# Computing the last 128 columns of a down projection transposed, with the weight stationary

## The chip, the cores and the metric

The kernel runs on one core of a Trainium2 chip. The metric is device time in microseconds (us) of one execution. A core has TensorE (matmuls; in the profile PE, and PEld for the loads of the stationary operand), VectorE (DVE), ScalarE (ACT), GpSimd (POOL) and SyncE (SP), each with an instruction queue of its own that is worked through in order, and 16 DMA engines. In this kernel nearly all DMAs are issued from SP's queue. TensorE writes to PSUM, which has 8 banks of 512 f32 columns; an instruction that needs what another engine makes waits on a semaphore.

## What is computed

Two branches over the same 2048 tokens of 640 columns are mixed by a gate per token. In outline (H = 32 heads of 20 columns):

```python
q, k, v = split(x @ wqkv)                       # per head
phi(t) = concat(softmax(t @ w_phi), softmax(-(t @ w_phi)))
num = phi(q) @ (phi(k)^T @ v);  den = phi(q) @ sum(phi(k))
a = concat_heads(num / (den + 1e-6)) @ wo
b = (silu(x @ w_gate) * (x @ w_up)) @ w_down    # 640 -> 1728 -> 640
g = sigmoid(sum(x * gate_w))
out = g * a + (1 - g) * b
```

The change is in how `b`'s last product, with `w_down`, is computed.

## The kernel before

**Tiling.** Tokens come in 16 tiles of 128 (`t`) and 4 blocks of 512 (`bt`). The 1728 inner columns of the feed-forward branch are 14 chunks of 128 (`k`; the last has 64).

*Gate and up* (`ffn`, lines 668 to 686): for a chunk and a block, five matmuls of 512 moving columns each for gate and for up, with the weight stationary and the transposed tokens `xT` moving. `ffn_tail` (640 to 666) turns them into `hT` (chunk on the partitions, tokens along the row): a tanh and a scaled copy `us` on ACT (line 456), a step on DVE (659), a product on POOL (665). `hT` has two buffers, one for even and one for odd blocks.

*Down* (`down`, lines 768 to 787): for each token tile, `hT`'s 128 tokens are stationary and `w_down` (`wd`) moves. The output is 640 columns wide, over two PSUM banks, so each of the 14 chunks is passed twice: 14 matmuls of 512 columns, then 14 of 128 columns. A down tile holds a pair of banks. The last tile's two parts are two tasks, so that the first can be finished while the second runs.

```python
        def part(j):
            return acc(bank(ctx["ps"], j, 0, P if j else 512),
                       [(hT[:, hb, k, tk], wd[:, k, 512:D] if j else wd[:, k, 0:512]) for k in range(NK)])
```

*K tiles and Q tiles* (`features`, 851 to 936): projections of a token tile (matmuls with `wkv` or `wq`), then per head a maximum and a minimum, two subtractions (lines 899 to 911, DVE), an exponential (ACT), a sum and a reciprocal (922, 926, DVE) and a normalization (932, POOL). K tiles feed `kvpart` (matmuls of `v1` and `phi`). A Q tile (`qtile`, 991 to 1039) goes on: a transposing DMA from SP (`qT`, phi to `eT`), a product with the summed keys and values (`num`, 11 narrow matmuls), a division on DVE (`den`, `o`: lines 1015, 1017, 1025), a transposing DMA (`oT`), and the product with `wo` (ten matmuls, half of them 128 columns wide).

*Output* (`finish`, `finals`, 730 to 766): the two branches meet in `xsb`, bf16. The one that comes first is scaled into `xsb` on ACT, for tiles below `B_FIRST` = 8 the feed-forward branch and from there on the attention branch. The second is added: for tiles below `FIN_DVE` = 12 by a scaled copy to `xb` on ACT (`evac`) and an add on POOL (`plus`, line 763), from tile 12 on by one DVE operation from PSUM (`fin`, line 749). Then SP issues the store of the tile. For the last tiles the down matmuls themselves wait for the first branch's store (line 745: `parts[0][0].deps.append(store_t[t])`).

**The order of work** is written by a planner when the kernel is built (`_Plan`, lines 236 to 337). Each piece of work is a task with an engine, a planned duration, a latency (`LAT`, line 246, the time until another engine may use it), dependences, a priority (lower goes first) and the buffers it takes and gives back (PSUM banks or pairs, `xb`, `eT`, `oT` and others). Whenever an engine is free in the plan, the task of lowest priority number that is ready and has its buffers is issued; it is never taken back. The engines then run their queues in that order, with semaphore waits. The planned durations set the order alone.

```python
    L_SLACK, E_SLACK, O_SLACK = 1.0, 1.8, 1.6
    K_AT, K_EACH, Q_AT, Q_EACH = 29.00, 6.158, 120.27, 8.184
```

`E_SLACK` and `O_SLACK` are added to the planned landing of a `qT` and an `oT` transfer; the second line says how early a K or Q tile's first matmul may stand in the plan. For TensorE `num` has priority 1, `wo` 1.5, K tiles 3, Q tiles 5; gate, up and down tiles have 10 and more and fill what is left, in the order of the list `seq` (lines 1051 to 1062): in blocks 2 and 3 the four down tiles of the block before are put one by one behind the gate and up pairs from the sixth on; the last two down tiles of block 2 are put behind all gate and up pairs (`late`), and the four of block 3 at the end.

Of the kernel before, what the change touches and what calls it, by code (L numbers as in the profile page):

```python
# [6 lines left out]
P = 128  # L7
S_TOK = 2048
D = 640
# [231 lines left out]
class _Plan:  # L241
# [11 lines left out]
    def add(self, eng, cost, fn, deps=(), prio=5.0, lat=None, acq=(), rel=(), name=""):  # L253
        t = _Task(eng, cost, fn, deps, prio, self.LAT[eng] if lat is None else lat,
                  tuple(acq), tuple(rel), len(self.tasks), name)
        self.tasks.append(t)
        return t
# [82 lines left out]
def _mm(*cols):  # L340
    return sum(c / 2400.0 + 0.003 for c in cols)


def _build(
# [22 lines left out]
    def sb(name, shape, dtype):  # L367
        t = nc.alloc_sbuf_tensor(name, list(shape), dtype)
        tr.reg_tensor(t, "sbuf", nc.lookup_mloc(t).addr, rowelems(shape), mybir.dt.size(dtype))
        return t  # L370

    def sbat(name, shape, dtype, at):
        t = nc.alloc_sbuf_tensor_at(name, list(shape), dtype, offset=at)
        tr.reg_tensor(t, "sbuf", at, rowelems(shape), mybir.dt.size(dtype))
        return t
# [8 lines left out]
    hT = sb("hT", [P, 2, NK, 512], BF16)  # L384
    us = sb("us", [P, 3, 512], BF16)
    phi = sb("phi", [P, NPHI, NG, P], BF16)
    v1 = sb("v1", [P, 8, VW], BF16)
    eT = sb("eT", [P, 2, NG, P], BF16)
    olab = nc.alloc_sbuf_tensor("olab", [P, 2 * OW + 2 * D], BF16)
    obase = nc.lookup_mloc(olab).addr  # L390
# [26 lines left out]
    x2 = A_x[0]  # L417
    out2 = out[0]

    plan = _Plan({"bank": 8, "phi": NPHI, "st": 3, "eT": 2, "ob": 2, "oT": 2, "us": 3, "dn": 2, "xb": 2, "pp": 2})  # L420
    add = plan.add

    def bank(i, j, c0, c1, r0=0, r1=P):
        return ps[r0:r1, (2 * i + j) * 512 + c0:(2 * i + j) * 512 + c1]
# [4 lines left out]
    def wide(i, n=D):  # L429
        return ps[:, 2 * i * 512:2 * i * 512 + n]  # L430
# [19 lines left out]
    def acc(o, pairs):  # L450
        n = len(pairs)
        return [(o, l, r, i == 0, i == n - 1) for i, (l, r) in enumerate(pairs)]

    def actop(o, i, func, scale=1.0):
        reads = [i] + ([scale] if isinstance(scale, bass.AP) else [])
        run("act", lambda: act.activation(o, i, func, scale=scale), reads=reads, writes=[o])  # L456
# [4 lines left out]
    def poolop(fn, reads, writes):  # L461
        run("pool", fn, reads=reads, writes=writes)
# [7 lines left out]
    def dma(eng, dst, src, transpose=False, keep=False):  # L470
        eobj = tr.engobj[eng]
        reads = [src] if src.tensor.name in tr.addr else []
        writes = [dst] if dst.tensor.name in tr.addr else []
        fn = (lambda: eobj.dma_start(dst, src, transpose=True)) if transpose else (lambda: eobj.dma_start(dst, src))
        ev = run(eng, fn, reads=reads, writes=writes, semname="dma")
        if keep:
            out_evs.append(ev)
# [151 lines left out]
    gate_t = {}  # L629
    mult_t = {}  # L630
    down_t = {}

    def w_dep(k):
        col = P * k
# [33 lines left out]
    def ffn(bt, k, rank):  # L668
        tsl = slice(512 * bt, 512 * bt + 512)
        ctx = {}  # L670
        before = [down_t.get((bt - 2, u)) for u in range(4)]
        w_ = w_dep(k)
        if k == 13:
            gu = add("pe", _mm(*[512] * 5), lambda: mms(acc(one(ctx["g"], 0, 512),
                      [(wg[:, c, 1664:1792], xT[:, c, tsl]) for c in range(5)])),
                      deps=before + [xl[bt], wgl[NPC], wul[NPC]], prio=rank, acq=[("bank", ctx, "g")], name="gu")
            ffn_tail(bt, k, ctx, (gu, gu), 0)
            return
        g_ = add("pe", _mm(*[512] * 5), lambda: mms(acc(one(ctx["g"], 0, 512),
                 [(wg[:, c, P * k:P * k + P], xT[:, c, tsl]) for c in range(5)])),  # L680
                 deps=before + [xl[bt], wgl[w_]], prio=rank, acq=[("bank", ctx, "g")], name="gate")
        u_ = add("pe", _mm(*[512] * 5), lambda: mms(acc(one(ctx["u"], 0, 512),
                 [(wu[:, c, P * k:P * k + P], xT[:, c, tsl]) for c in range(5)])),
                 deps=[wul[w_]], prio=0.0, acq=[("bank", ctx, "u")], name="up")
        u_.after = g_
        ffn_tail(bt, k, ctx, (g_, u_), 0)
# [40 lines left out]
    pend = []  # L727
    wq_done = [None]

    def finish(t, which, ctx, dep):  # L730
        sc = gs[:, 0 if which == "a" else 1, t:t + 1]
        x_ = xsb[:, t, :]
        rel = [("pair", ctx, "ps")]
        if (t < B_FIRST) == (which == "b"):
            store_t[t] = add("act", 0.69, lambda: actop(x_, wide(ctx["ps"]), ACTF.Copy, scale=sc),
                             deps=[dep, gs_t[t // 4], wq_done[0]], prio=1, rel=rel, name=which + "st")
        else:
            pend.append((t, sc, ctx, dep, rel))

    def finals():  # L740
        for t, sc, ctx, dep, rel in pend:
            x_ = xsb[:, t, :]
            if t >= FIN_DVE:
                parts = dep if isinstance(dep, list) else [(dep, 0, D)]
                parts[0][0].deps.append(store_t[t])
                for d_, c0, c1 in parts:
                    def fin(x_=x_[:, c0:c1], ctx=ctx, sc=sc, c0=c0, c1=c1):
                        p_ = wide(ctx["ps"], c1)[:, c0:c1]
                        dveop(lambda: dve.scalar_tensor_tensor(out=x_, in0=p_, scalar=sc, in1=x_, op0=ALU.mult, op1=ALU.add),  # L749
                              [p_, sc, x_], [x_])  # L750
                    f = add("dve", 0.14 + 0.00105 * (c1 - c0), fin, deps=[d_, store_t[t], gs_t[t // 4]], prio=0.5,
                            rel=rel if c1 == D else (), name="fin")
                    add("sp", 0.33, lambda x_=x_, t=t, c0=c0, c1=c1: dma("sp", out2[t * P:(t + 1) * P, c0:c1], x_[:, c0:c1], keep=True),
                        deps=[f], prio=1, name="out")
                continue
            else:
                dep.deps.append(store_t[t])
                e = add("act", 0.69, lambda ctx=ctx, sc=sc: actop(xb[:, ctx["xb"], :], wide(ctx["ps"]), ACTF.Copy, scale=sc),
                        deps=[dep, gs_t[t // 4]], prio=1, acq=[("xb", ctx, "xb")], rel=rel, name="evac")

                def plus(x_=x_, ctx=ctx):
                    b_ = xb[:, ctx["xb"], :]
                    poolop(lambda: pool.tensor_tensor(x_, x_, b_, ALU.add), [x_, b_], [x_])
                f = add("pool", 1.35, plus, deps=[e, store_t[t]], prio=0.5, rel=[("xb", ctx, "xb")], name="plus")
            add("sp", 0.33, lambda x_=x_, t=t: dma("sp", out2[t * P:(t + 1) * P, :], x_, keep=True),
                deps=[f], prio=1, name="out")

    def down(bt, u, rank):
        t = 4 * bt + u
        ctx = {}  # L770
        hb = bt % 2
        tk = slice(P * u, P * u + P)

        def part(j):
            return acc(bank(ctx["ps"], j, 0, P if j else 512),
                       [(hT[:, hb, k, tk], wd[:, k, 512:D] if j else wd[:, k, 0:512]) for k in range(NK)])
        hold = {"deps": [mult_t[bt, k] for k in range(NK)] + wd_l, "prio": rank, "acq": [("pair", ctx, "ps")], "name": "down"}
        if t < NT - 1:
            d_ = add("pe", _mm(*([512] * 14 + [128] * 14)), lambda: mms(part(0) + part(1)), **hold)
            down_t[bt, u] = d_  # L780
            return t, ctx, d_
        first = add("pe", _mm(*[512] * 14), lambda: mms(part(0)), **hold)
        second = add("pe", _mm(*[128] * 14), lambda: mms(part(1)), prio=0.0, name="down")
        second.after = first
        down_t[bt, u] = second
        return t, ctx, [(first, 0, 512), (second, 512, D)]

    def premult(which, wT_l, prio, step=0.0, at=0.0):  # L790
        ev = []
# [260 lines left out]
    seq += [("f", k, 0) for k in range(K_PAIRS, NK)]  # L1052
    for bt in range(1, NBT):
        ks = list(range(K_PAIRS if bt == 1 else 0, NK))
        ds = [("d", u, bt - 1) for u in range(4)]
        for i, k in enumerate(ks):
            seq.append(("f", k, bt))
            if i >= D_AFTER and ds:
                seq.append(ds.pop(0))
        seq += ds  # L1060
    late = [e for e in seq if e[0] == "d" and e[2] == NBT - 2][2:]
    seq = [e for e in seq if e not in late] + late + [("d", u, NBT - 1) for u in range(4)]
    downs = []
    for i, (kind, j, bt) in enumerate(seq):
        if kind == "f":
            ffn(bt, j, 10.0 + 0.01 * i)
        else:
            downs.append(down(bt, j, 10.0 + 0.01 * i))
    for t in range(NT):
# [57 lines left out]
```

## Time and profile before

| what | value |
|---|---|
| median of 3 runs | 286.96 us (286.87 to 287.4) |
| the profiled execution's own time | 287.4 us |
| its span, first to last instruction | 285.7 us |
| granted TensorE clock | 1.000 |
| down matmuls (line 446, `ps<-wd,hT`) | 224 of 512 columns, 224 of 128 columns |
| issue to landing, median: `eT`, `oT` transposes | 3.6 us, 2.6 us |

Lines of the profile read like this: start or group, engine (PE, PEld, DVE, ACT, POOL, SPq for SP's DMA issues), source line, operation, output<-input by the program's names, shapes as partitions x elements, and a count. A matmul's recorded length includes its way through the array; matmuls follow each other more closely than that, so the distance of two starts is what one costs. Matmuls all carry line 446 and many ACT operations line 456, since a helper records them; tiles' names tell them apart. In the page's second part each digit is a 40th of the span, in tenths.

### The profile page before, as it was taken

To read this page: it belongs to the slowest core of one execution; us is meant where nothing else is said; L and a number is where in the kernel's file an instruction comes from. 1 tells how busy PE (TensorE), PEld (TensorE's weight loads), DVE (VectorE), ACT (ScalarE), POOL (GpSimd) and SP (SyncE) were. 2 spreads that over 40 slices of the span, in tenths; PEclk is the share of its full clock that TensorE was granted. 3 is DMA by queue.
4 is the path that set the end of the run, shared out by engine and by line. 5 is a ranking of instruction groups with operands and counts; after the bars stand their busy time and mean duration, and the time that the engine had idled before them with its cause. 6 is when DMAs were issued, how large, how long until landed. Compare 5 with 4: busy or idle time off the path is not lost.

```text
span 285.7 us, 5001 instructions
## 1 busy us (share of the span) xinstructions
PE 282.5 (99%) x1970; PEld 149.6 (52%) x1970; DVE 223.4 (78%) x318; ACT 149.1 (52%) x238; POOL 171.6 (60%) x168
## 2 busy tenths in 40 slices
PE   8999999999999999999999999999999999999996
PEld 3445554555554555654455656555554555555654
DVE  1323449998999797799999999999979979962312
ACT  2455655886676564436636444566664653562210
POOL 5099633749478635456784485589898458638100
PEclk9999999999999999999999999999999999999999
DMA  7979997920000000000002483744375245363211
GB/s 171 271 120 246 214 245 129 334 86 0 0 2 0 0 2 0 2 0 2 0 2 52 76 125 77 109 112 94 69 144 70 55 83 118 70 76 73 71 46 46
DMA packets 68112, 24.22 MB, mean 85 GB/s; under 512 B 56249, under 2 KB 68089, under 8 KB 68089
## 3 DMA queue, kind: packets, MB, share of 16 engines
q1 hardware_dynamic: 67433, 23.91, 40.1%
q8 instruction: 15, 0.25, 0.4%
q10 hardware_dynamic: 656, 0.00, 0.1%
q14 instruction: 8, 0.07, 0.1%
HBM read 8.30 MB, written 2.62 MB: 38 GB/s over the span
## 4 chain that ended last, share of the span: by engine, by line
PE 99%; DVE 0%; issue 0%
PE ps L446 97%; PE ps L619 2%; DVE xsb L749 0%
## 5 line engine op out<-in xcount | busy, mean ns | idle before, releaser
L665 POOL TENSOR_TENSOR hT<-hT,us 128x512 bf16<-128x512 bf16 (+1 forms) x56 | 64.1, 1154 | 53.1 <-DVE hT L659 31.1
L932 POOL TENSOR_TENSOR phi<-phi,rc 128x1320 bf16<-128x1320 bf16 x32 | 77.6, 2426 | 28.8 <-DVE rc L926 26.0
L446 PE MATMUL ps<-xT,wg 128*128 128x512 bf16 x280 | 69.7, 381 | 0.0
L446 PE MATMUL ps<-xT,wu 128*128 128x512 bf16 x260 | 64.3, 379 | 0.0
L446 PE MATMUL ps<-wd,hT 128*128 128x512 bf16 (+1 forms) x448 | 63.0, 299 | 0.0
L922 DVE TENSOR_REDUCE sm<-phi 128x66 f32<-128x1320 bf16 x32 | 48.5, 1519 | 10.6 <-ACT phi L456 10.6
L659 DVE SCALAR_TENSOR_TENSOR hT<-hT,ps 128x512 bf16<-128x512 bf16 (+1 forms) x56 | 37.6, 676 | 22.8 <-ACT hT L456 22.7
L456 ACT ACTIVATE hT<-ps 128x512 bf16<-128x512 f32 (+1 forms) x56 | 33.2, 597 | 40.7 <-PE ps L446 40.3
L456 ACT ACTIVATE phi<-phi 128x1320 bf16<-128x1320 bf16 x32 | 41.7, 1304 | 22.2 <-DVE phi L911 22.2
L446 PEld LDWEIGHTS ps<-wd,hT 128*128 128x128 bf16 x448 | 35.0, 98 | 27.4
L446 PE MATMUL ps<-wkv,xT 128*128 128x289 bf16 (+2 forms) x240 | 45.8, 343 | 0.0
L456 ACT ACTIVATE us<-ps 128x512 bf16<-128x512 f32 (+1 forms) x56 | 33.2, 597 | 16.4 <-PE ps L446 14.2
L446 PEld LDWEIGHTS ps<-xT,wu 128*128 128x128 bf16 x260 | 25.3, 98 | 30.8 <-ACT phi L456 0.4
L446 PEld LDWEIGHTS ps<-xT,wg 128*128 128x128 bf16 x280 | 26.0, 98 | 27.9 <-issue 1.5
L446 PEld LDWEIGHTS ps<-wkv,xT 128*128 128x128 bf16 x240 | 22.9, 97 | 18.4
L899 DVE TENSOR_REDUCE mx<-ps 128x33 f32<-128x660 f32 x32 | 26.6, 833 | 3.4 <-PE ps L446 3.3
L911 DVE TENSOR_TENSOR phi<-mn,ps 128x660 bf16<-128x660 f32 x32 | 26.4, 824 | 0.3
L903 DVE TENSOR_REDUCE mn<-ps 128x33 f32<-128x660 f32 x32 | 26.5, 828 | 0.0
L907 DVE TENSOR_TENSOR phi<-ps,mx 128x660 bf16<-128x660 f32 x32 | 26.5, 827 | 0.0
L456 ACT ACTIVATE xsb<-ps,gs 128x640 bf16<-128x640 f32 x16 | 12.7, 793 | 24.7 <-PE ps L446 24.7
L446 PE MATMUL ps<-wq,xT 128*128 128x512 bf16 (+1 forms) x160 | 24.3, 299 | 0.0
L446 PE MATMUL ps<-wo,oT 128*128 128x512 bf16 (+1 forms) x160 | 24.3, 299 | 0.0
(47 smaller groups left out, 184.9 us busy)
## 6 DMA issues: line engine op xcount, KB each, us to landing
out_dram<-xsb SPq DMA_DIRECT2D x15, 160.0 KB, 1.8
wd<-in_B_w_down_dram SPq DMA_DIRECT2D x1, 2080.0 KB, 9.3
wg<-in_B_w_gate_dram SPq DMA_DIRECT2D x2, 400.0 KB, 5.3
wu<-in_B_w_up_dram SPq DMA_DIRECT2D x2, 400.0 KB, 6.5
wo<-in_A_wo_dram SPq DMA_DIRECT2D x1, 800.0 KB, 10.0
wg<-in_B_w_gate_dram SPq DMA_DIRECT2D x2, 320.0 KB, 4.7
wu<-in_B_w_up_dram SPq DMA_DIRECT2D x2, 320.0 KB, 5.6
wkv<-in_A_wqkv_dram SPq DMA_DIRECT2D x1, 600.0 KB, 4.4
```

The costliest lines, as they stand in the source:

```text
L446: last = pe.matmul(o, lhsT=l, rhs=r, start=st, stop=sp_, skip_group_check=True)
L456: run("act", lambda: act.activation(o, i, func, scale=scale), reads=reads, writes=[o])
L619: last = pe.matmul(one(b, 0, 512), lhsT=ones_row[:, 0:P], rhs=ones_row[:, 0:512], start=True, stop=True, skip_group_check=True)
L659: dveop(lambda: dve.scalar_tensor_tensor(out=hap, in0=hap, scalar=1.0, in1=g_, op0=ALU.add, op1=ALU.mult), [hap, g_], [hap])
L665: poolop(lambda: pool.tensor_tensor(hap, hap, u_, ALU.mult), [hap, u_], [hap])
L899: dveop(lambda: dve.tensor_reduce(a, b, AX.X, ALU.max), [b], [a])
L903: dveop(lambda: dve.tensor_reduce(a, b, AX.X, ALU.min), [b], [a])
L907: dveop(lambda: dve.tensor_tensor(o_, a, b, ALU.subtract), [a, mx[:, ctx["st"], :]], [o_])
L911: dveop(lambda: dve.tensor_tensor(o_, a, b, ALU.subtract), [b, mn[:, ctx["st"], :]], [o_])
L922: dveop(lambda: dve.tensor_reduce(a, b, AX.X, ALU.add), [b], [a])
L932: poolop(lambda: pool.tensor_tensor(a, a, b, ALU.mult), [a, r], [a])
```

## The change

The 128 columns 512 to 639 of the down projection are taken out of the down tiles. For each block a new TensorE task `rest` computes them transposed: the 128-column slice of `wd` is stationary and 512 tokens of `hT` move, 14 matmuls into one bank. ACT copies the result to `xb` as bf16 (`rcp`), SP issues a transposing DMA of four 128x128 blocks (`turn`), which for blocks 0 and 1 goes straight to `xsb` and is scaled there by the gate on POOL (`rsc`), and for blocks 2 and 3 to a new buffer `rX`, from which a DVE operation of 128 columns per tile (`more`) adds it. `rX` shares its memory with `v1`. A down tile now has 14 matmuls of 512 columns, in one bank; the last tile's two parts are 384 and 128 columns wide. Copies, adds and finals of the feed-forward branch shrink from 640 to 512 columns. The last tile's columns 512 to 639 are stored by a DMA of their own. `rest` stands ahead of its block's down tiles in `seq`, and `hT` is free for block `bt` only when `rest` of `bt - 2` is done too. The planner's constants stay.

```diff
@@ -384,7 +384,11 @@
     hT = sb("hT", [P, 2, NK, 512], BF16)
     us = sb("us", [P, 3, 512], BF16)
     phi = sb("phi", [P, NPHI, NG, P], BF16)
-    v1 = sb("v1", [P, 8, VW], BF16)
+    vlab = nc.alloc_sbuf_tensor("vlab", [P, 8 * VW], BF16)
+    vbase = nc.lookup_mloc(vlab).addr
+    assert vbase % 32 == 0, vbase
+    v1 = sbat("v1", [P, 8, VW], BF16, vbase)
+    rX = sbat("rX", [P, 2, 4, P], BF16, vbase)
     eT = sb("eT", [P, 2, NG, P], BF16)
     olab = nc.alloc_sbuf_tensor("olab", [P, 2 * OW + 2 * D], BF16)
     obase = nc.lookup_mloc(olab).addr
@@ -417,7 +421,7 @@
     x2 = A_x[0]
     out2 = out[0]
 
-    plan = _Plan({"bank": 8, "phi": NPHI, "st": 3, "eT": 2, "ob": 2, "oT": 2, "us": 3, "dn": 2, "xb": 2, "pp": 2})
+    plan = _Plan({"bank": 8, "phi": NPHI, "st": 3, "eT": 2, "ob": 2, "oT": 2, "us": 3, "dn": 2, "xb": 2, "rX": 2, "pp": 2})
     add = plan.add
 
     def bank(i, j, c0, c1, r0=0, r1=P):
@@ -629,6 +633,8 @@
     gate_t = {}
     mult_t = {}
     down_t = {}
+    rest_t = {}
+    rest_x = {}
 
     def w_dep(k):
         col = P * k
@@ -668,7 +674,7 @@
     def ffn(bt, k, rank):
         tsl = slice(512 * bt, 512 * bt + 512)
         ctx = {}
-        before = [down_t.get((bt - 2, u)) for u in range(4)]
+        before = [down_t.get((bt - 2, u)) for u in range(4)] + [rest_t.get(bt - 2)]
         w_ = w_dep(k)
         if k == 13:
             gu = add("pe", _mm(*[512] * 5), lambda: mms(acc(one(ctx["g"], 0, 512),
@@ -727,43 +733,91 @@
     pend = []
     wq_done = [None]
 
+    DM = 512
+
     def finish(t, which, ctx, dep):
         sc = gs[:, 0 if which == "a" else 1, t:t + 1]
-        x_ = xsb[:, t, :]
-        rel = [("pair", ctx, "ps")]
+        n = D if which == "a" else DM
+        x_ = xsb[:, t, 0:n]
+        rel = [("pair", ctx, "ps")] if which == "a" else [("bank", ctx, "ps")]
+
+        def src():
+            return wide(ctx["ps"]) if which == "a" else one(ctx["ps"], 0, DM)
         if (t < B_FIRST) == (which == "b"):
-            store_t[t] = add("act", 0.69, lambda: actop(x_, wide(ctx["ps"]), ACTF.Copy, scale=sc),
-                             deps=[dep, gs_t[t // 4], wq_done[0]], prio=1, rel=rel, name=which + "st")
+            store_t[t] = add("act", 0.11 + 0.0009 * n, lambda: actop(x_, src(), ACTF.Copy, scale=sc),
+                             deps=[dep if which == "a" else dep[0][0], gs_t[t // 4], wq_done[0]], prio=1, rel=rel, name=which + "st")
         else:
-            pend.append((t, sc, ctx, dep, rel))
+            pend.append((t, n, sc, ctx, dep, rel, src))
 
     def finals():
-        for t, sc, ctx, dep, rel in pend:
-            x_ = xsb[:, t, :]
+        for t, n, sc, ctx, dep, rel, src in pend:
+            last = []
             if t >= FIN_DVE:
-                parts = dep if isinstance(dep, list) else [(dep, 0, D)]
-                parts[0][0].deps.append(store_t[t])
-                for d_, c0, c1 in parts:
-                    def fin(x_=x_[:, c0:c1], ctx=ctx, sc=sc, c0=c0, c1=c1):
-                        p_ = wide(ctx["ps"], c1)[:, c0:c1]
+                dep[0][0].deps.append(store_t[t])
+                for d_, key, c0, c1 in dep:
+                    def fin(x_=xsb[:, t, c0:c1], ctx=ctx, key=key, sc=sc, n=c1 - c0):
+                        p_ = one(ctx[key], 0, n)
                         dveop(lambda: dve.scalar_tensor_tensor(out=x_, in0=p_, scalar=sc, in1=x_, op0=ALU.mult, op1=ALU.add),
                               [p_, sc, x_], [x_])
                     f = add("dve", 0.14 + 0.00105 * (c1 - c0), fin, deps=[d_, store_t[t], gs_t[t // 4]], prio=0.5,
-                            rel=rel if c1 == D else (), name="fin")
-                    add("sp", 0.33, lambda x_=x_, t=t, c0=c0, c1=c1: dma("sp", out2[t * P:(t + 1) * P, c0:c1], x_[:, c0:c1], keep=True),
+                            rel=[("bank", ctx, key)], name="fin")
+                    last.append((f, c0, c1))
+            else:
+                d_ = dep if n == D else dep[0][0]
+                d_.deps.append(store_t[t])
+                e = add("act", 0.11 + 0.0009 * n, lambda ctx=ctx, sc=sc, n=n, src=src: actop(xb[:, ctx["xb"], 0:n], src(), ACTF.Copy, scale=sc),
+                        deps=[d_, gs_t[t // 4]], prio=1, acq=[("xb", ctx, "xb")], rel=rel, name="evac")
+
+                def plus(x_=xsb[:, t, 0:n], ctx=ctx, n=n):
+                    b_ = xb[:, ctx["xb"], 0:n]
+                    poolop(lambda: pool.tensor_tensor(x_, x_, b_, ALU.add), [x_, b_], [x_])
+                f = add("pool", 0.2 + 0.0018 * n, plus, deps=[e, store_t[t]] + ([rest_x[t // 4]] if n == D else []), prio=0.5,
+                        rel=[("xb", ctx, "xb")], name="plus")
+                last.append((f, 0, n))
+            if n < D:
+                def more(x_=xsb[:, t, DM:D], r_=lambda t=t: rX[:, rest_c[t // 4]["rX"], t % 4, :], sc=sc):
+                    b_ = r_()
+                    dveop(lambda: dve.scalar_tensor_tensor(out=x_, in0=b_, scalar=sc, in1=x_, op0=ALU.mult, op1=ALU.add),
+                          [b_, sc, x_], [x_])
+                m = add("dve", 0.25, more, deps=[rest_x[t // 4], store_t[t], gs_t[t // 4]], prio=1.45,
+                        rel=[("rX", rest_c[t // 4], "rX")] if t % 4 == 3 else (), name="more")
+                c0, c1 = last[0][1], last[0][2]
+                last = [(f, c0, c1, [m] if i == 0 else []) for i, (f, c0, c1) in enumerate(last)]
+            else:
+                last = [(f, c0, c1, []) for f, c0, c1 in last]
+            if t == NT - 1:
+                add("sp", 0.33, lambda t=t: dma("sp", out2[t * P:(t + 1) * P, DM:D], xsb[:, t, DM:D], keep=True), deps=[m], prio=1, name="out")
+                for f, c0, c1, _ in last:
+                    add("sp", 0.33, lambda t=t, c0=c0, c1=c1: dma("sp", out2[t * P:(t + 1) * P, c0:c1], xsb[:, t, c0:c1], keep=True),
                         deps=[f], prio=1, name="out")
-                continue
             else:
-                dep.deps.append(store_t[t])
-                e = add("act", 0.69, lambda ctx=ctx, sc=sc: actop(xb[:, ctx["xb"], :], wide(ctx["ps"]), ACTF.Copy, scale=sc),
-                        deps=[dep, gs_t[t // 4]], prio=1, acq=[("xb", ctx, "xb")], rel=rel, name="evac")
-
-                def plus(x_=x_, ctx=ctx):
-                    b_ = xb[:, ctx["xb"], :]
-                    poolop(lambda: pool.tensor_tensor(x_, x_, b_, ALU.add), [x_, b_], [x_])
-                f = add("pool", 1.35, plus, deps=[e, store_t[t]], prio=0.5, rel=[("xb", ctx, "xb")], name="plus")
-            add("sp", 0.33, lambda x_=x_, t=t: dma("sp", out2[t * P:(t + 1) * P, :], x_, keep=True),
-                deps=[f], prio=1, name="out")
+                add("sp", 0.33, lambda t=t: dma("sp", out2[t * P:(t + 1) * P, :], xsb[:, t, :], keep=True),
+                    deps=[last[0][0]] + last[0][3], prio=1, name="out")
+
+    rest_c = {}
+
+    def rest(bt, rank):
+        ctx = {}
+        rest_c[bt] = ctx
+        hb = bt % 2
+        first = 4 * bt < B_FIRST
+        r_ = add("pe", _mm(*[512] * NK), lambda: mms(acc(one(ctx["ps"], 0, 512), [(wd[:, k, DM:D], hT[:, hb, k, :]) for k in range(NK)])),
+                 deps=[mult_t[bt, k] for k in range(NK)] + wd_l, prio=rank, acq=[("bank", ctx, "ps")], name="rest")
+        rest_t[bt] = r_
+        e = add("act", 0.49, lambda: actop(xb[:, ctx["xb"], 0:512], one(ctx["ps"], 0, 512), ACTF.Copy), deps=[r_], prio=1,
+                acq=[("xb", ctx, "xb")], rel=[("bank", ctx, "ps")], name="rcp")
+        xs_ = xsb[:, 4 * bt:4 * bt + 4, DM:D]
+
+        def turn():
+            dma("sp", xs_ if first else rX[:, ctx["rX"], :, :], xb[:, ctx["xb"], 0:512], transpose=True)
+        x_ = add("sp", 1.3, turn, deps=[e, wq_done[0]], prio=0.5, lat=2.1, acq=() if first else [("rX", ctx, "rX")], rel=[("xb", ctx, "xb")], name="rX")
+        x_.slack = E_SLACK
+        if first:
+            def scaled():
+                g_ = gs[:, 1, 4 * bt:4 * bt + 4]
+                poolop(lambda: pool.tensor_tensor(xs_, xs_, g_.unsqueeze(2).to_broadcast([P, 4, P]), ALU.mult), [xs_, g_], [xs_])
+            x_ = add("pool", 1.1, scaled, deps=[x_, gs_t[bt]], prio=0.6, name="rsc")
+        rest_x[bt] = x_
 
     def down(bt, u, rank):
         t = 4 * bt + u
@@ -771,21 +825,18 @@
         hb = bt % 2
         tk = slice(P * u, P * u + P)
 
-        def part(j):
-            return acc(bank(ctx["ps"], j, 0, P if j else 512),
-                       [(hT[:, hb, k, tk], wd[:, k, 512:D] if j else wd[:, k, 0:512]) for k in range(NK)])
-        hold = {"deps": [mult_t[bt, k] for k in range(NK)] + wd_l, "prio": rank, "acq": [("pair", ctx, "ps")], "name": "down"}
+        def part(key, c0, c1):
+            return lambda: mms(acc(one(ctx[key], 0, c1 - c0), [(hT[:, hb, k, tk], wd[:, k, c0:c1]) for k in range(NK)]))
+        hold = {"deps": [mult_t[bt, k] for k in range(NK)] + wd_l, "prio": rank, "name": "down"}
         if t < NT - 1:
-            d_ = add("pe", _mm(*([512] * 14 + [128] * 14)), lambda: mms(part(0) + part(1)), **hold)
+            d_ = add("pe", _mm(*[DM] * NK), part("ps", 0, DM), acq=[("bank", ctx, "ps")], **hold)
             down_t[bt, u] = d_
-            return t, ctx, d_
-        first = add("pe", _mm(*[512] * 14), lambda: mms(part(0)), **hold)
-        second = add("pe", _mm(*[128] * 14), lambda: mms(part(1)), prio=0.0, name="down")
+            return t, ctx, [(d_, "ps", 0, DM)]
+        first = add("pe", _mm(*[384] * NK), part("ps", 0, 384), acq=[("bank", ctx, "ps"), ("bank", ctx, "p2")], **hold)
+        second = add("pe", _mm(*[128] * NK), part("p2", 384, DM), prio=0.0, name="down")
         second.after = first
         down_t[bt, u] = second
-        return t, ctx, [(first, 0, 512), (second, 512, D)]
-
-
+        return t, ctx, [(first, "ps", 0, 384), (second, "p2", 384, DM)]
 
     def premult(which, wT_l, prio, step=0.0, at=0.0):
         ev = []
@@ -1052,18 +1103,20 @@
     seq += [("f", k, 0) for k in range(K_PAIRS, NK)]
     for bt in range(1, NBT):
         ks = list(range(K_PAIRS if bt == 1 else 0, NK))
-        ds = [("d", u, bt - 1) for u in range(4)]
+        ds = [("r", 0, bt - 1)] + [("d", u, bt - 1) for u in range(4)]
         for i, k in enumerate(ks):
             seq.append(("f", k, bt))
             if i >= D_AFTER and ds:
                 seq.append(ds.pop(0))
         seq += ds
     late = [e for e in seq if e[0] == "d" and e[2] == NBT - 2][2:]
-    seq = [e for e in seq if e not in late] + late + [("d", u, NBT - 1) for u in range(4)]
+    seq = [e for e in seq if e not in late] + late + [("r", 0, NBT - 1)] + [("d", u, NBT - 1) for u in range(4)]
     downs = []
     for i, (kind, j, bt) in enumerate(seq):
         if kind == "f":
             ffn(bt, j, 10.0 + 0.01 * i)
+        elif kind == "r":
+            rest(bt, 10.0 + 0.01 * i)
         else:
             downs.append(down(bt, j, 10.0 + 0.01 * i))
     for t in range(NT):
```

## The prediction

> **What bounds the kernel now.** I read the page from the top (busy shares, the 40 slices, the chain that ended last), then the timeline of TensorE for its real cadence, then busy time by stretches and the other engines' timelines for what could make TensorE wait.
>
> ```profile
> span 285.7 us, 5001 instructions
> PE 282.5 (99%) x1970; PEld 149.6 (52%) x1970; DVE 223.4 (78%) x318; ACT 149.1 (52%) x238; POOL 171.6 (60%) x168
> PEclk9999999999999999999999999999999999999999
> PE 99%; DVE 0%; issue 0%
> ```
>
> The chain that ended last is TensorE alone, at full granted clock. Busy time says little about pipelined matmuls, so their starts must be read (start, length, what):
>
> ```profile
> 256.20 1.24 PE L446 MATMUL ps<-xT,wg 128*128 128x512 bf16 x5
> 257.28 7.77 PE L446 MATMUL ps<-wd,hT 128*128 128x512 bf16 x56
> 264.89 1.52 PE L446 MATMUL ps<-wo,oT 128*128 128x512 bf16 x10
> 266.25 0.48 PE L446 MATMUL ps<-kvsb,eT 128*128 128x63 bf16 x11
> 266.56 7.77 PE L446 MATMUL ps<-wd,hT 128*128 128x512 bf16 x56
> 274.17 1.52 PE L446 MATMUL ps<-wo,oT 128*128 128x512 bf16 x10
> 275.53 7.77 PE L446 MATMUL ps<-wd,hT 128*128 128x512 bf16 x56
> ```
>
> Five 512-column matmuls take 257.28 - 256.20 = 1.08 us, 216 ns each. Ten for wo, half of them 128 columns wide, take 266.25 - 264.89 = 1.36, so a narrow one costs 0.28 / 5 = 56 ns. Two down tiles (28 wide, 28 narrow) should be 28 x 0.272 = 7.62; they take 274.17 - 266.56 = 7.61. So nothing waits here, and a matmul costs 0.417 ns a column ((216 - 56) / 384) plus 56 - 53.3 = 2.7 ns. Weight loads are hidden even behind narrow ones. The same holds wherever I compared starts from 7.4 us to the last matmul's end at 283.3.
>
> ```profile
> 150.00:160.00 10.00, 10.00 (x82) 5.73 (x81) 9.96 (x15) 5.28 (x6) 4.22 (x6) 1.00 0.39 73
> 220.00:230.00 10.00, 10.00 (x69) 5.16 (x67) 9.93 (x16) 5.78 (x8) 5.52 (x5) 1.00 0.46 63
> 250.00:260.00 10.00, 10.00 (x65) 5.02 (x64) 6.69 (x11) 6.14 (x9) 5.25 (x4) 1.00 0.50 62
> ```
>
> Columns: stretch, its length, then busy time of PE, weight loads, DVE, ACT, POOL. VectorE is nearly full too from 100 to 250 us: a second limit right behind the first. TensorE has no gap to close; the change can only shorten its sum or open gaps.
>
> **What is removed and added on TensorE.** Before: 16 tiles x 14 x (216 + 56) = 60.93 us. After: four rest groups of 14 wide, 56 x 216 = 12.10; fifteen down tiles of 14 wide, 210 x 216 = 45.36; the last tile as 14 x 384 columns (0.417 x 384 + 2.7 = 163 ns, 2.28) and 14 x 128 (0.78). Sum 60.52. The columns streamed are the same; 154 fewer matmuls save 2.7 ns each: **0.4 us**, all on the path. All 224 narrow loads go and 56 come, hidden both ways.
>
> At this place the Trainium skill ("TensorE: Matmul & The Clock Gate", Back-to-back issue gap) says that in a stream of load and matmul pairs a 128-column matmul takes about 81 ns and a 512-column one about 131. By it the estimate would be 224 x 81 - 56 x 131 = 10.8 us of gain; this trace has 56 and 216 ns for these very pairs and disagrees.
>
> **The copy (rcp), ACT.** Four 128x512 PSUM copies at 597 ns (the us copy's row): +2.4 us. Twelve stores or evacuations shrink from 640 to 512 columns: between the 793 and 597 ns rows, I take 690: -1.2. Net +1.2 us on an engine 52% busy. Each rcp waits for its rest group; behind it queue tanh, us and exp, and so VectorE and POOL.
>
> **The turn, SP queue.** Four DMA transposes of four blocks; the five-block oT transpose holds the queue 1.21 us and lands 2.6 us after issue, the eleven-block eT 1.39 and 3.6. I take 1.2 and 2.6: 4.8 us of queue time in all, and one more output issue of 0.33. A turn waits for rcp in order; behind it are qT, oT and output issues, and behind those TensorE's num and wo. The plan lets readers in 5.2 us after the turn begins (1.3 + 2.1 + 1.8), twice what the row needs. DMA is half idle there: hidden.
>
> **rsc and plus, POOL.** Two scalings of 128x512, between 0.94 (the 1320-column norm's 2426 ns, scaled) and 1.15 (hT multiply): 2.3 us; four adds shrink from 1.40 to about 1.15: -1.0. Hidden at 60% busy; behind rsc are hmul and norm.
>
> **more, VectorE.** Eight 128x128 operations, between 179 ns (33 columns) and 350 (the 128-column final from PSUM): I take 300, 2.4 us; three finals shrink from 884 to 751. Only tiles 8 to 11, 1.2 us, come before the last Q tile's work at 258. The cover is VectorE's idle time, 3.9 us waiting for exp in 225 to 262. If that is gone, Q tile 14 and 15 come up to 1.2 us later.
>
> **Banks and order.** A down tile takes one PSUM bank instead of a pair, so more is free: a gain in slack, not in time, since TensorE never idles. But the plan, which picks TensorE's order, will pick another from 99 us on. Slack there is thin: at 126.58 a K tile's matmuls start, and the subtraction that frees their banks ends only 0.40 us earlier:
>
> ```profile
> 125.34 0.84 DVE L911 TENSOR_TENSOR phi<-mn,ps 128x660 bf16<-128x660 f32 x1
> 126.58 2.87 PE L446 MATMUL ps<-wkv,xT 128*128 128x289 bf16 x15
> ```
>
> Plan errors that now just fit may not fit in another order. Cost of this: at least 0 (there is no idle to win back), at most the lateness of one VectorE chain, about 1.2 us, since one stall moves TensorE behind everything later. I take 0.1, nearer to zero, as the present order has stalls of only about 0.05.
>
> **The end.** The last piece is again 128 columns: 0.35 us final, its issue and landing. The first piece's final is shorter and frees SP earlier, worth at most 0.05; I take 0. The rest group of block 3 waits for the same products as the first down of block 3 did: the last product ended about 261.7, TensorE gets there about 265.
>
> **Sum.** The profiled execution took 287.4 us (285.7 span, 1.7 around it), 0.4 above the median of 286.96. 287.4 - 0.4 + 0.1 = 287.1 for it; on the median, **286.6 us**.
>
> **Rivals.** (1) A hole before the last down (slower). The last down waits for ACT's store of tile 15, which follows wo of tile 15. Now that wo stands ahead of the last two downs, and the third hides the store:
>
> ```profile
> 275.73 0.80 ACT L456 ACTIVATE xsb<-ps,gs 128x640 bf16<-128x640 f32 x1 [8.49 <-PE ps L446]
> ```
>
> The code's planning numbers (they set order; prices are from the trace) keep wo 5.95 us or more behind num of tile 15. Two downs with their narrow halves covered that (7.6); two without are planned as 6.06. If the rest group of block 3 goes ahead of num, its turn holds SP just when oT wants it, by some 0.1 us, and that margin is gone: the planner then takes the third down before wo, and the last down waits 0.2 (matmul end to ACT) + 0.80 + 0.05 = 1.05 us. It decides where num of tile 15 is not yet allowed when wo of tile 14 is done. For it: block 2's rest group moves 3.02 - 2 x 0.78 = 1.5 us ahead of the late downs, then those are 1.56 shorter, so TensorE arrives at about 266, as before; num was started at 266.25, nearly as soon as allowed (eT issued at 260.61 and the plan's 5.4). Against: either order of a few tenths flips it. Time: 286.6 + 1.05 = 287.6.
>
> (2) Stalls in the middle (slower): the four added operations and the new order push VectorE late for TensorE somewhere in 99 to 260 us. For: 9.9 of 10 us busy. Against: fewer banks held, and shorter filler groups (3.02 instead of 3.81 us) let K and Q tiles start sooner. Price 0.5 to 2 us, middle 1.2: 287.8.
>
> (3) The skill's pair rate holds for these matmuls (faster): 286.96 - 10.8 = 276. The 56 and 216 ns rows are almost conclusive against.
>
> (4) The rest group comes too early and waits for block 3's products: TensorE reaches it about 3 us after they are done; counted in (2).
>
> **How the numbers follow.** Forecast 0.48, of which 0.08 lies under 286.4 (gain, 0.05 at the end, the old 0.05 stall, scatter of 0.1); rival 1 0.30, of which 0.21 over 287.5; rival 2 (with 4) 0.20, of which 0.17 over; rival 3 0.02. A measurement of this kernel can tell 0.2%, 0.57 us, from nothing: faster 0.10, same 0.52, slower 0.38. The likeliest case alone spans 286.3 to 287.0; with both slower rivals the range is 286.3 to 288.2, leaving out rival 3 and the worst of rival 2.
>
> **What the profile would show.** TensorE: 1816 matmuls, down groups of 3.02 us, no narrow ones but the last 14; its stream ends about 0.3 us earlier. ACT: four copies of 0.6; SP: four transposes landing in about 2.6; VectorE eight operations of about 0.3. Rival 1: TensorE idle 1 us before its last 28 matmuls, released by ACT; rival 2: a matmul group waiting on VectorE or ACT between 99 and 260 us, and the chain no longer TensorE alone. Wrong altogether if wide matmuls with w_down loaded run off 216 ns, or if the transposes land late enough to hold VectorE or SP.

## The result and the profile after

The changed kernel takes 286.34 us (median of 11), the kernel before 287.11 beside it: ratio 0.9974, 95% interval 0.9966 to 0.9982. A second comparison, among the experiments, gave 286.47 against 286.91, ratio 0.9982 (0.9973 to 0.9991). The profiled execution of the changed kernel took 286.7 us, that of the kernel before 287.4. So it is faster, by about 0.2%, and by more than the 0.3 us that the forecast's sum had.

The page of the changed kernel, the lines that answer to those shown of before:

```profile
span 285.0 us, 4720 instructions
PE 281.9 (99%) x1816; PEld 143.4 (50%) x1816; DVE 225.8 (79%) x326; ACT 150.2 (53%) x242; POOL 172.4 (61%) x170
PEclk9999999999999999999999999999999999999999
PE 99%; DVE 0%; issue 0%
```

1816 matmuls instead of 1970, as worked out, and still the chain is TensorE alone. TensorE's timeline at the end (start, length, what):

```profile
261.42 3.19 PE L450 MATMUL ps<-wd,hT 128*128 128x512 bf16 x14
264.44 0.48 PE L450 MATMUL ps<-kvsb,eT 128*128 128x63 bf16 x11
264.76 1.52 PE L450 MATMUL ps<-wo,oT 128*128 128x512 bf16 x10
266.12 3.19 PE L450 MATMUL ps<-hT,wd 128*128 128x512 bf16 x14
269.14 3.19 PE L450 MATMUL ps<-wd,hT 128*128 128x512 bf16 x14
272.17 1.52 PE L450 MATMUL ps<-wo,oT 128*128 128x512 bf16 x10
273.52 9.26 PE L450 MATMUL ps<-wd,hT 128*128 128x512 bf16 x56
```

A down tile is 264.44 - 261.42 = 3.02 us, the rest group (`ps<-hT,wd`) 269.14 - 266.12 = 3.02: 216 ns a matmul with either operand stationary. Every group starts where the matmuls before it leave TensorE, with no gap. The product `num` of tile 15 (264.44) stands ahead of the rest group (266.12), so the order of the first rival did not come about.

Where the time went, by the two profiles. TensorE's stream is taken from the start of the first group of up matmuls, since the time before it depends on the first loads and scatters (that group came at 7.42 and 6.82 us in two profiles of the kernel before, at 7.35 and 6.74 in two of the changed one).

| stretch | before | after | difference |
|---|---|---|---|
| first up group to the last matmul's end | 7.42 to 283.30: 275.88 | 7.35 to 282.79: 275.44 | -0.44 |
| of it: one stall, at 138 us | 0.05 | none | -0.05 |
| last matmul's end to the end of the span | 2.38 | 2.16 | -0.22 |

That is -0.39 from the matmul count, -0.05 from the stall, -0.22 from the end: 0.66 us, 0.23%, inside both intervals. The remaining 0.11 us of the first comparison's 0.77 lies within its interval (0.52 to 0.98 us).

The end is read from SP's timeline, the last two stores together and the last one alone (the last matmul ends at 282.79):

```profile
282.69 0.85 SPq L478 DMA_DIRECT2D out_dram<-xsb  x2
```

```profile
283.20 0.33 SPq L478 DMA_DIRECT2D out_dram<-xsb  x1
```

### The profile page after: what moved, and what is told of

It is laid out like the page before. It is cut to its first block, busy times and chain, and to the rows that moved or that the text cites. A ratio compares the mean times of both kernels' runs of the same rounds, so it can differ in the third digit from the quotient of the medians.

```text
span 285.0 us, 4720 instructions
## 1 busy us (share of the span) xinstructions
PE 281.9 (99%) x1816; PEld 143.4 (50%) x1816; DVE 225.8 (79%) x326; ACT 150.2 (53%) x242; POOL 172.4 (61%) x170
## 4 chain that ended last, share of the span: by engine, by line
PE 99%; DVE 0%; issue 0%
PE ps L450 97%; PE ps L623 2%; DVE xsb L760 0%
## 5 line engine op out<-in xcount | busy, mean ns | idle before, releaser
L450 PE MATMUL ps<-wd,hT 128*128 128x512 bf16 (+2 forms) x238 | 50.7, 366 | 0.0
L450 PEld LDWEIGHTS ps<-wd,hT 128*128 128x128 bf16 x238 | 22.4, 98 | 24.0
L460 ACT ACTIVATE xsb<-ps,gs 128x512 bf16<-128x512 f32 (+1 forms) x16 | 11.9, 741 | 27.3 <-PE ps L450 27.2
```

The source lines that it names most:

```text
L450: last = pe.matmul(o, lhsT=l, rhs=r, start=st, stop=sp_, skip_group_check=True)
```

## Experiments

My theory: TensorE's stream stays gapless, each matmul saved is worth a fixed time, and the end is shorter because of the last stores. Rivals: the gain comes from order or banks, or the shorter end is chance.

**The changed kernel again.**

> The changed kernel, unaltered, timed beside the kernel before and the three kernels below. If the gain beyond TensorE's sum is real, it is 0.6 to 0.9 us faster than the kernel before again, and from the end of the last matmul to the end of the span it takes about 2.1 us, against 2.35 in the profile of the kernel before. If that part was scatter of one profile, it is about 0.45 us faster (matmul count and the old stall) and the end takes 2.3 to 2.4.

Measured: 286.47 against 286.91, ratio 0.9982 (0.9973 to 0.9991), 0.44 us. The median is at the second expectation (0.45), but the interval (0.26 to 0.77 us) reaches into the first and does not separate them. Its profile does: the stream from 6.74 to 282.18 is 275.44 us again, and the end is 2.17.

**The rest group with 128 tokens at a time** (168 matmuls more, everything else as in the changed kernel).

```diff
-acc(one(ctx["ps"], 0, 512), [(wd[:, k, DM:D], hT[:, hb, k, :]) for k in range(NK)])
+sum([acc(one(ctx["ps"], P * u, P * u + P),
+         [(wd[:, k, DM:D], hT[:, hb, k, P * u:P * u + P]) for k in range(NK)]) for u in range(4)], [])
```

> The changed kernel with the rest group's 14 matmuls of 512 tokens cut into 56 of 128 tokens; same output, same planned order, 168 matmuls more. Theory (the gain on TensorE is 2.7 ns for each matmul saved): the stream is 168 x 2.7 = 0.45 us longer than in the changed kernel, and so is the time. Rival (the gain comes from order, banks or the end): under 0.1 us. By the pair rate of about 81 ns for a 128-column matmul (the Trainium skill, TensorE: Matmul & The Clock Gate, Back-to-back issue gap) an estimate would be 224 x 81 - 56 x 216 = 6 us longer.

Measured: 286.85 us, ratio to before 0.9994 (0.9985 to 1.0003), 0.38 above the changed kernel beside it. Timeline of TensorE, the rest group and its neighbours:

```profile
265.16 1.52 PE L450 MATMUL ps<-wo,oT 128*128 128x512 bf16 x10
266.52 3.29 PE L450 MATMUL ps<-hT,wd 128*128 128x128 bf16 x56
269.65 3.19 PE L450 MATMUL ps<-wd,hT 128*128 128x512 bf16 x14
```

The 56 narrow matmuls take 269.65 - 266.52 = 3.13 us, 55.9 ns each, against 3.02 for 14 wide ones over the same columns: 0.11 us a block. The stream is 7.43 to 283.29, 275.86, 0.42 longer, 2.5 ns for each of the 168. This undoes just the matmul count, and the gain on TensorE is gone with it. By the rate of about 81 ns that the Trainium skill ("TensorE: Matmul & The Clock Gate", Back-to-back issue gap) gives for a 128-column matmul in a stream of load and matmul pairs, the estimate was 6 us longer. The 55.9 ns and 0.42 us of this run disagree with that rate, and the measurement decides.

**Down tiles holding a pair of banks** as before the change, using one of them.

```diff
-            d_ = add("pe", ..., part("ps", 0, DM), acq=[("bank", ctx, "ps")], **hold)
+            ctx = _Even()     # ctx["ps"] is twice the pair's number; the pair is given back where the bank was
+            d_ = add("pe", ..., part("ps", 0, DM), acq=[("pair", ctx, "pr")], **hold)
```

> The changed kernel with its down tiles holding a pair of banks, as before the change, while using only one (tiles 0 to 14). The prediction said that the freed bank is slack and not time: then within 0.2 us of the changed kernel. Rival: with the rest group and its copy in the loop, pairs are short, and TensorE has nothing it may start; the planned order has holes of about 0.6 us at 157, 0.5 at 182, 0.5 at 198 and 0.2 at 162, 1.75 us in all: then 1 to 2 us slower than the changed kernel, about 1 us slower than the kernel before.

Measured: 289.73 us, ratio 1.0096 (1.0083 to 1.0109), 3.3 us above the changed kernel. Timeline of TensorE around three of the holes (in brackets the idle time and what ended it):

```profile
195.31 1.24 PE L455 MATMUL ps<-xT,wu 128*128 128x512 bf16 x5
196.39 0.48 PE L455 MATMUL ps<-kvsb,eT 128*128 128x63 bf16 x11
197.25 2.33 PE L455 MATMUL ps<-xT,wg 128*128 128x512 bf16 x10 [0.37 <-ACT us L465]
```

```profile
234.40 1.24 PE L455 MATMUL ps<-xT,wu 128*128 128x512 bf16 x5
236.20 1.52 PE L455 MATMUL ps<-wo,oT 128*128 128x512 bf16 x10 [0.56 <-DVE dn L1072]
237.55 1.52 PE L455 MATMUL ps<-wq,xT 128*128 128x512 bf16 x10
239.60 1.68 PE L455 MATMUL ps<-wd,hT 128*128 128x512 bf16 x7 [0.53 <-DVE hT L670]
```

Eleven narrow matmuls of `num` need 0.32 us, but the gate group behind them starts 0.86 later: the trace puts the wait down to ACT's copy `us`, which empties a bank. There are seven such holes, each ending within 0.15 us of an ACT or DVE operation that reads a bank. They add up to 3.4 us, twice what was planned. So the freed bank is not spare room that may be given back: with the rest group in the loop, the gapless stream rests on it. The kernel before had pairs and no holes, but no rest groups; what pairs alone cost there was not tried.

**The kernel before, with the changed kernel's last tile** (the edit in outline).

```diff
-        first = ... part(0) (columns 0 to 511);   second = ... part(1) (columns 512 to 639)
+        zero = ... columns 512 to 639;   first = ... columns 0 to 383
+        second = ... columns 384 to 511, in a bank of its own
```

> The kernel before with only its last token tile done as in the changed kernel's end: columns 512 to 639 first, then 0 to 383, then 384 to 511, each with its final and its store; 14 matmuls more. Theory (the changed kernel's shorter end comes from the first piece's store being issued before the last final): TensorE ends 0.04 us later and the stretch from there to the end of the span is about 0.2 us shorter, 0.15 us faster than the kernel before in all. Rival (the end differed by scatter): 0.04 us slower, the end 2.3 to 2.4 us.

Measured: 286.72 us, ratio 0.9994 (0.9985 to 1.0003), 0.19 us below the kernel before; the interval includes no change. The profile is plainer. SP's timeline of the last two stores, and of the last one alone, first in the kernel before (its last matmul ends at 283.30):

```profile
283.39 0.82 SPq L474 DMA_DIRECT2D out_dram<-xsb  x2
```

```profile
283.76 0.44 SPq L474 DMA_DIRECT2D out_dram<-xsb  x1
```

and here (its last matmul ends at 283.21):

```profile
283.11 0.85 SPq L474 DMA_DIRECT2D out_dram<-xsb  x2
```

```profile
283.62 0.33 SPq L474 DMA_DIRECT2D out_dram<-xsb  x1
```

Before (times from the last matmul's end), the first piece's 751 ns final ended just as the last matmul did, its store went out at +0.09 us, and the last store followed back to back, at +0.46, and held the queue for 0.44 us. With a first piece of 384 columns (617 ns) the store is out at -0.10, and the last one goes at +0.41 and takes 0.33. The end shrinks from 2.38 to 2.19 us (2.16 in the changed kernel), with nothing else of the change in place. This trace also has a pair of stores with 0.10 us between them (SP's timeline, each alone):

```profile
280.32 0.33 SPq L474 DMA_DIRECT2D out_dram<-xsb  x1
```

```profile
280.75 0.38 SPq L474 DMA_DIRECT2D out_dram<-xsb  x1
```

The second one's 0.38 us lies between the 0.44 with 0.04 us between them and the 0.33 with 0.18, although the store ahead of it is the widest of the three, 640 columns against 512 and 384. So the longer issue goes with the distance and not with the width of the store ahead.

**Two stores back to back in the changed kernel**: the last tile cut at 448 instead of 384 columns.

```diff
-        first = add("pe", _mm(*[384] * NK), part("ps", 0, 384), ...)
-        second = add("pe", _mm(*[128] * NK), part("p2", 384, DM), ...)
+        first = add("pe", _mm(*[448] * NK), part("ps", 0, 448), ...)
+        second = add("pe", _mm(*[64] * NK), part("p2", 448, DM), ...)
```

> The changed kernel with the last tile cut into 448 and 64 columns instead of 384 and 128. The first final (about 0.68 us) now outlasts the second piece's matmuls (14 x 29 ns), so the second final (about 0.28) waits for it and the last two stores are issued back to back again. Theory (a store issued right behind another takes 0.44 us to issue instead of 0.33, whatever its width): the last store begins about 0.7 us after the last matmul's end, takes 0.44, and the end of the span is about 2.6 us after that matmul. Rival (the narrower first store made the end shorter, not the spacing): the last store takes 0.33 and the end about 2.45.

Measured in one profile (SP's timeline, the last store alone):

```profile
283.01 0.43 SPq L478 DMA_DIRECT2D out_dram<-xsb  x1
```

The last store begins 0.72 us after the last matmul's end (282.29) and 0.04 after the store before it, holds the queue for 0.43, and the span ends 2.56 after that matmul. The store of 64 columns paid the longer issue too, so it is the spacing and not the store's own width. The kernel's time of 286.56 is one execution and says no more.

**Tile 15's `num` planned later.**

```diff
-        tT.slack = E_SLACK
+        tT.slack = E_SLACK + (2.0 if t == NT - 1 else 0.0)
```

> The changed kernel with 2.0 us more of planned slack on the transfer ahead of tile 15's num, so that the planner puts block 3's rest group ahead of it. By the prediction's first rival the planner then takes three of the last four downs before tile 15's wo, and the last down waits for ACT's store: TensorE idle 1.05 us at about 280.5, time 1.05 us above the changed kernel, 287.4. If the end has more give than that (the real wo is done sooner than planned), under 0.5 us.

Measured: 287.53 us, ratio 1.0014 (1.0005 to 1.0023), 0.9 to 1.2 above the changed kernel by ratios (1.0014 against 0.9982 and 0.9974). Timeline of TensorE:

```profile
265.67 3.19 PE L450 MATMUL ps<-hT,wd 128*128 128x512 bf16 x14
268.69 0.48 PE L450 MATMUL ps<-kvsb,eT 128*128 128x63 bf16 x11
269.01 9.23 PE L450 MATMUL ps<-wd,hT 128*128 128x512 bf16 x42
278.08 1.52 PE L450 MATMUL ps<-wo,oT 128*128 128x512 bf16 x10
280.49 3.23 PE L450 MATMUL ps<-wd,hT 128*128 128x384 bf16 x28 [0.89 <-ACT xsb L460]
```

and, from the chain that ended last, what lies between (start, length, what):

```profile
279.64 0.80 ACT xsb L460
280.44 0.05 issue
280.49 3.25 PE ps L450 x28
```

Three downs now precede `wo` of tile 15, and the last down stands behind ACT's store: the ten matmuls of `wo` leave TensorE at 279.44, the next starts at 280.49, 1.05 us later. It is the first rival as priced. By the planner's own times, 1.5 us of added slack still leaves `num` ahead of the rest group (it only changes places with `wo` of tile 14), and 2.0 puts it behind.

**Added DVE work four times over** for tiles 8 to 11.

```diff
                 def more(...):
                     b_ = r_()
+                    for _ in range(3 if t < 12 else 0):
+                        dveop(lambda: dve.scalar_tensor_tensor(out=b_, in0=b_, scalar=1.0, in1=b_, op0=ALU.mult, op1=ALU.max), [b_], [b_])
```

> The changed kernel with three further 128x128 operations on DVE ahead of each added one of tiles 8 to 11 (they write back what they read), 12 x 0.35 = 4.2 us of DVE work between 225 and 250 us, not known to the planner, so in the same order. Theory (added DVE work is covered by idle time and slack; num and wo have 2 to 3 us between landing and use there): under 0.5 us slower than the changed kernel. Rival (DVE is a second limit right behind TensorE): 2 to 4 us slower, with TensorE waiting on DVE or on transfers behind it.

Measured: 288.98 us, ratio 1.0068 (1.0051 to 1.0085), 2.5 to 2.7 us above the changed kernel by ratios (against 0.9982 and 0.9974). From DVE's groups and from TensorE's timeline in 225 to 262 us:

```profile
L781 DVE SCALAR_TENSOR_TENSOR rX<-rX 128x128 bf16<-128x128 bf16 x12 | 3.6, 296 | 0.3
```

```profile
242.68 1.52 PE L450 MATMUL ps<-wo,oT 128*128 128x512 bf16 x10
245.32 1.52 PE L450 MATMUL ps<-wq,xT 128*128 128x512 bf16 x10 [1.11 <-DVE dn L1069]
```

```profile
252.21 1.24 PE L450 MATMUL ps<-xT,wu 128*128 128x512 bf16 x5
253.99 0.48 PE L450 MATMUL ps<-kvsb,eT 128*128 128x63 bf16 x11 [0.54 <-DVE phi L965]
```

3.6 us more of DVE work cost TensorE 2.3 us in four stalls (the `wq` group comes 1.28 us late, the `num` group 0.70). Only about 1.3 us was covered. DVE is a second limit right behind TensorE, and the rival holds for this dose. The change's own four operations there, 1.4 us, were in place in both kernels and still fitted, so the 1.3 us is what was left beyond them.

**The kernel before again**, for a second profile.

> The kernel before, for a second profile of its end and its start. If the shorter end of the changed kernel is real, the stretch from the last matmul's end to the end of the span is again about 2.35 us here, and about 2.1 in every profile of the changed kernel. The start (to the second group of gate matmuls, 7.42 us in the first profile) is expected to scatter by some 0.1 us.

Measured: the last matmul ends at 282.92, the span at 285.29, 2.37 us later, with the last store again 0.46 behind the matmul's end and 0.44 long. The five profiles of the changed kernel and of its variants with the same last stores (narrow rest, pairs, late `num`, more DVE work, the kernel again) have 2.16 or 2.17. The start scattered more than expected: 6.82 us against 7.42. The stream from the first up group on is 276.10 us here, against 275.88; 0.21 of that is two stalls at 8.70 and 10.05 us, near the start, and the one at 138 us is there again.

## Why the prediction came out as it did

*The matmul count* (predicted 0.4 us) was right: 0.39 in the profile, and 0.42 came back when 168 matmuls were put back. The fixed cost per matmul is 2.5 ns; 2.7 came from rounding. Of the weight loads, 210 narrow ones go and not 224, since the last tile keeps 14 narrow matmuls; the 154 saved in all was right.

*The end* was the term that was mis-sized. The prediction said the earlier store was "worth at most 0.05; I take 0". It measured 0.21 to 0.22. I had seen only that the last store's issue started 45 ns late behind the one before, and that part is as large as the bound. The issue itself was also 0.11 us longer for following back to back, and its data landed another 0.06 later, counted from the issue's end (1.17 us against 1.10 to 1.12 in the changed kernel); what makes up these last 0.06 stays open. The line that carried the 0.11 was in the profile: the two last stores on SP, 0.44 us for the second where others took 0.33.

*Stalls* (0.1 us taken) were none: the old one of 0.05 went too, and no run tells why. With the end, this makes 0.66 us where the sum said 0.3 (286.96 - 0.3 = 286.66). Both terms erred the same way, so the 286.34 us stands 0.04 above the lower end of the range, among the times under 286.4 that had a chance of 0.08; "faster" had 0.10. The mechanism was right; that the number is still inside the range owes something to luck.

*"A gain in slack, not in time"*, of the freed bank, was wrong as a reading of the change: its other half, the rest group, cannot do without it in this order of work. Giving the pair back costs 3.3 us.

*The first rival* did not happen, though its mechanism was right, and its price (1.05 us). The step that failed in it was when `num` of tile 15 would be allowed. I took it from the kernel before (transfer issued at 260.61). In the new order Q tile 15's matmuls started at 243.97 instead of 245.01 and its transfer went out at 258.91, 1.7 us sooner, so `num` went ahead of the rest group.

*The second rival* had its premise right: beyond the 1.4 us that the added work took, DVE had about 1.3 us to give there. The added operation was priced at 300 ns and took 349, just the upper bound's 350. Why the 1.4 fitted stays open. The new order starts the last two Q tiles 3.3 and 1.0 us sooner, but the two before them 4.0 and 3.6 later.

*The hidden costs* stayed hidden and near their rows: the copy 587 ns (597 taken), the 512-column stores 688 (690), the scaling on POOL 1040 (between 940 and 1150), the transposes 2.5 to 2.6 us from issue to landing (2.6).

## What to carry to other kernels

When a kernel is one gapless stream on TensorE and the columns streamed stay the same, price a rearrangement by the number of matmuls times the fixed cost of one (here 2.5 ns), and then look at the two places where the stream is not the time: the last stores, and what buffers the new piece of work must find free. A busy engine behind the bound has a reserve that can be measured by adding work to it (here about 1.3 us beyond the change's own); an addition has to be compared with that, not with the engine's idle share. An order made by a planner can flip on a shift of one due time (here by 2.0 us), and a flip at the end can cost a whole store (here 1.05 us).

## What was unexpected of the hardware

A store issued within 0.05 us of the end of the one before it on SP's queue held the queue for 0.43 to 0.44 us instead of 0.33, in both profiles of the kernel before and when the last tile was cut at 448 columns; with 0.10 us between them it took 0.38, and with 0.18 it took 0.33. Right behind a transposing DMA the queue is held longer still: in the first profile of the kernel before, full-width stores issued 0.05 us behind an `oT` transpose took 0.58 us, and behind an `eT` transpose 0.77 to 0.78. The changed last tile, with its last two stores apart, ends the kernel 0.2 us sooner after the last matmul.
